# Sigmoid attention and an MLP mixer in one kernel: when keys are regrouped, and in which order keys, queries and values are loaded

## The chip, the cores and the metric

The kernel runs on one core of a Trainium2 chip. The metric is the device time of one execution in microseconds (us), as the median of several runs. An engine's name is shortened as in the profile: PE is the matmul engine, DVE the vector engine, ACT the scalar engine, POOL the general engine (it issues the loads here), SP the engine that issues stores and transposing transfers. All transfers are moved by the core's 16 DMA engines.

## The reference

For 8 batches of 12 heads, with 448 positions of 64 numbers per head, attention with a sigmoid in place of the softmax; the heads are then laid side by side (768 columns) and pass a token mixing and a channel mixing layer.

```
scores = scale * np.matmul(q, k.transpose(0, 1, 3, 2)) - np.log(S)
attn = 1.0 / (1.0 + np.exp(-scores))
x = np.matmul(attn, v)                      # then heads side by side: (8, 448, 768)
xt = x.transpose(0, 2, 1)
h = np.maximum(xt @ w_tok1, 0.0) @ w_tok2   # token mixing, 448 -> 256 -> 448
u = x + h.transpose(0, 2, 1)
h2 = np.maximum(u @ w_ch1, 0.0) @ w_ch2     # channel mixing, 768 -> 1536 -> 768
return u + h2
```

## The kernel before

Batches are counted from 0 to 7. The 12 heads of a batch are worked off in three units of four heads (u = 0, 1, 2), so there are 24 cycles, c = 3b + u. The order of all instructions on all engines is written out by hand: each engine's queue runs in the order in which the program names its instructions.

A cycle c does three things for three different units. `qk` (line 179) forms seven blocks of scores of unit c, each block followed by a sigmoid on ACT (line 191). `av` (line 201) multiplies the sigmoids of unit c - 1 with its values into two PSUM banks, 0 and 1, called xa; DVE copies them to the tile xT (line 220), and `xtrans_dma` (line 235) transposes xT through a transfer on SP to the tile xn. `tok_tail` and `tok1` (lines 260 and 278) do the first token product of unit c - 2 from its xn, and `ytrans` (line 305) the second into two banks, again 0 and 1, called yt; DVE adds them to xT and writes the tile ut (line 319). So the `av` of a cycle takes the banks that the `ytrans` at the end of the cycle before it used, once DVE has emptied them.

Between these pieces stand the products of the channel layer of earlier batches. From c = 9 on a cycle holds a third of the second channel product of batch b - 2 (lines 367 and 605); its results are added up by DVE (`o`, line 564) and stored by SP. At the end of a batch's third cycle stands the first channel product of batch b - 1 (`sevens`, line 1045, matmuls at line 491). In cycles 6 to 8 the second channel product of batch 0 stands in their place, cut into pieces that `work(share)` (line 1066) hands out in three portions a cycle. Each piece is followed by one entry of the list `copies`, if there is one, else by one of the list `early` (sums of weights on DVE, line 409).

Queries and keys reach PE in four steps. A load on POOL converts them to half precision into raw_q and raw_k (line 115). `relayout` (line 120) is a copy on DVE, one for each unit, from raw to rel (line 126). `dma_transpose` (line 138) is one transfer on SP for all three units of a batch, to the tile tr, from which `qk` reads. `through_dma(b, 0)` (line 144) makes a list of eight entries from it: three copies of k, the transpose of k, three copies of q, the transpose of q. In the loop from line 1120 the function `some(n)` runs the next n entries of that list. It is called twice in a cycle: with `within` after the third block of scores, and with `behind` after the second channel product and ahead of `ytrans`. Values need no regrouping: `av` reads raw_v.

`gated_loads(b)` (line 969) holds the loads back: a tiny copy on POOL reads the last element of the transposed queries of batch b + 1, and the loads stand behind it in POOL's queue. It is called at the end of cycles 5 and 8, inside cycle 11, and at the end of the second cycle of batches 4 to 6. raw_k and raw_q have one buffer each for these batches, raw_v has two.

In cycle 7 the list `copies` takes k's four entries ahead of the cycle's second portion of work (line 1097), in cycle 8 q's four entries after the third block of scores (line 1089).

Of the kernel before, what the change touches and what calls it, by code (L numbers as in the profile page):

```python
# [23 lines left out]
NU = 3  # L24
# [6 lines left out]
def kernel(  # L31
# [13 lines left out]
    B, H, S, E = q.shape  # L45
# [39 lines left out]
    def bank(shape, dtype, name):  # L85

        if opening_banks:
            n = opening_banks.pop(0)
        else:
            n = at_bank[0]  # L90
            at_bank[0] = (n + 1) % 4
        return pp.tile(shape, dtype, tag=f"m{n}", bufs=1, name=name)
# [7 lines left out]
    def raw_tile(b, t):  # L100
        if (b, t) not in raw:
            tag, bufs = f"raw_{t}", 2 if t == "v" else 1
            if b == 1 and t != "v":
                tag = f"rel_{t}"
            raw[b, t] = pa.tile(
                [128, NU, 2, NJ, E], FP16, tag=tag, bufs=bufs, name=f"raw_{t}_{b}"
            )
        return raw[b, t]

    def load(b, t, src, u0, u1):  # L110

        for g in range(2):
            dst = raw_tile(b, t)[64 * g : 64 * g + 64, u0:u1, :, :, :]
            heads = src[b, 6 * g + 2 * u0 : 6 * g + 2 * u1]
            nc.gpsimd.dma_start(
                out=dst.rearrange("p u hi j e -> p (u hi) (j e)"),
                in_=heads.rearrange("h (p j) e -> p h (j e)", j=NJ),
            )

    def relayout(b, t, u):  # L120

        if (b, t) not in rel:
            rel[b, t] = pa.tile(
                [128, NU, NJ, 2, E], FP16, tag=f"rel_{t}", bufs=1, name=f"rel_{t}_{b}"
            )
        nc.vector.tensor_copy(
            out=rel[b, t][:, u, :, :, :],
            in_=raw[b, t][:, u, :, :, :].rearrange("p hi j e -> p j hi e"),
        )
# [8 lines left out]
    def dma_transpose(b, t, u0, u1=NU):  # L138
        nc.sync.dma_start_transpose(
            out=tr_tile(b, t)[:, u0:u1, :, :].rearrange("e u j r -> e (u j) r"),  # L140
            in_=rel[b, t][:, u0:u1, :, :, :].rearrange("r u j hi e -> r (u j hi e)"),
        )

    def through_dma(b, u0):

        pieces = []
        for t in ("k", "q"):
            for u in range(u0, NU):
                pieces.append(lambda t=t, u=u: relayout(b, t, u))
            pieces.append(lambda t=t: dma_transpose(b, t, u0))  # L150
        return pieces

    def by_unit(b, u0):

        pieces = []
        for u in range(u0, NU):
            for t in ("k", "q"):
                pieces.append(lambda t=t, u=u: relayout(b, t, u))
            for t in ("k", "q"):
                pieces.append(lambda t=t, u=u: dma_transpose(b, t, u, u + 1))  # L160
        return pieces
# [73 lines left out]
    def xtrans_dma(b, u):  # L235
        nc.sync.dma_start_transpose(
            out=xn_tile(b, u).rearrange("s g t d -> s (g t) d"),
            in_=xTs[b % 2][:, u, :, :].rearrange("d g s -> d (g s)"),
        )
# [65 lines left out]
    def ytrans(b, u, banks=()):  # L305
        for g in range(2):
            db = NU * g + u
            if banks:
                at_bank[0] = banks[g]
            ps = bank([128, 512], FP32, f"yt_{b}_{db}")  # L310
            for tcb in range(2):
                nc.tensor.matmul(  # L312
                    out=ps[:, 0:S],
                    lhsT=h1[b, u][:, tcb, g, :],
                    rhs=w2[:, tcb, :, :],
                    start=(tcb == 0),
                    stop=(tcb == 1),
                )
            nc.vector.tensor_tensor(  # L319
                out=uts[b % 2][:, db, 0:S], in0=xTs[b % 2][:, u, g, 0:S], in1=ps[:, 0:S], op=ADD  # L320
            )
# [531 lines left out]
    def pieces_ch2(b, groups):  # L853
        for t, half in groups:
            for n in range(0, NCB, 3):
                yield 3 * DH, lambda t=t, half=half, n=n: ch2(b, t, half, n, n + 3)

    def pieces_last(b):
        for n in range(0, NCB, 3):
            yield 3 * DH, lambda n=n: ch2_last(b, n, n + 3)  # L860
# [108 lines left out]
    def gated_loads(b):  # L969

        nc.gpsimd.tensor_copy(  # L971
            out=gate[:, :], in_=tr[b + 1, "q"][:, NU - 1, NJ - 1, 126:128]
        )
        if b > 1:
            load(b + 1, "v", v, 0, NU)
        for t, src in (("k", k), ("q", q)):
            if b + 2 < B:
                load(b + 2, t, src, 0, NU)

    ON_DMA = range(N_FIRST, N_CYCLES)  # L980

# [3 lines left out]
    for c, cb in ((N_FIRST, 3), (N_FIRST + 1, 8)):  # L985
        b, u = divmod(c, NU)
        before = divmod(c - 1, NU)
        ahead = divmod(c + 1, NU)
        copies = []
# [27 lines left out]
        if u == 2:  # L1017
            copies = by_unit(2, 1)
# [33 lines left out]
    pending, copies = [], []  # L1052
    early = weight_sums()
    lane = [0]
    for c in range(2 * NU, ONE_RUN):
        b, u = divmod(c, NU)
        before, ahead = divmod(c - 1, NU), divmod(c - 2, NU)


        if c == 2 * NU:  # L1060
            first = c
            pending, shares = [*pieces_ch2(0, by_half[2:]), *pieces_last(0)], [10, 10, 10]
            total = sum(w for w, f in pending)
            spent = 0

        def work(share):
            goal = 3 * sum(shares[: c - first]) + share * shares[c - first]
            done = 0
            while pending and spent + done < total * goal / 90:
                w, f = pending.pop(0)  # L1070
                if len(pending) % 4 == 3:
                    lane[0] ^= 1
                at_bank[0] = 2 + lane[0]
                f()
                done += w
                if copies:
                    copies.pop(0)()
                elif early:
                    early.pop(0)()
            return done  # L1080

        qk(b, u, 0)
        qk(b, u, 1)
        at_bank[0] = 0
        av(*before)
        xtrans_dma(*before)
        qk(b, u, 2)
        if c == 2 * NU + 2:
            copies += through_dma(3, 0)[NU + 1 :]
        spent += work(1)  # L1090
        qk(b, u, 3)
        qk(b, u, 4)
        at_bank[0] = 0
        tok_tail(*ahead)
        tok1(*ahead, with_scores=True)
        if c == 2 * NU + 1:
            copies = through_dma(3, 0)[: NU + 1]
        spent += work(2)
        if c == 2 * NU + 2:
            utrans(b - 1)  # L1100
            token_sums(b - 1)
        qk(b, u, 5)
        qk(b, u, 6)
        if u < 2:
            at_bank[0] = 0
            ytrans(*ahead)
        spent += work(3)
        if u == 2:
            sevens(b - 1)
            at_bank[0] = 0  # L1110
            ytrans(*ahead)
            gated_loads(b)
    assert not copies and not pending and not early

    def some(n):
        for f in copies[:n]:
            f()
        del copies[:n]

    for c in range(ONE_RUN, N_CYCLES):  # L1120
        b, u = divmod(c, NU)
        before, ahead = divmod(c - 1, NU), divmod(c - 2, NU)
        if b == NU:
            within, behind = ((0, 0), (4, 2), (2, 0))[u]
        else:
            within, behind = 2, 2
        if u == 0:
            assert not copies
            copies += through_dma(b + 1, 0) if b + 1 < B else output_sums()

        X, Y = 2, 0
        at_bank[0] = X
        turn0, turn1, rest = ch2_pair(b - 2, u)
        part = len(turn1) * 2 // 3
        qk(b, u, 0)
        qk(b, u, 1)
        for f in turn0:
            f()  # L1140
        qk(b, u, 2)
        some(within)
        if c == ONE_RUN + 2:
            gated_loads(b)
        if u == 2:
            utrans(b - 1)
        at_bank[0] = Y
        av(*before, 0, 4)
        qk(b, u, 3)
        av(*before, 4, NJ)  # L1150
        xtrans_dma(*before)
        if u == 2:
            token_sums(b - 1)
        qk(b, u, 4)
        for f in turn1[:part]:
            f()
        qk(b, u, 5)
        for f in turn1[part:]:
            f()
        at_bank[0] = Y  # L1160
        tok_tail(*ahead)
        qk(b, u, 6)
        tok1(*ahead, with_scores=True)
        rest()
        some(behind)
        if u == 1 and NU < b < B - 1:
            gated_loads(b)
        if u == 2:
            at_bank[0] = Y + 1
            for w, f in pieces_last(b - 2):  # L1170
                f()
            sevens(b - 1)
        at_bank[0] = Y
        ytrans(*ahead)
# [93 lines left out]
```

## Time and profile before

| | |
|---|---|
| median of 3 runs | 347.46 us (347.26 to 347.76) |
| the profiled execution | 347.11 us |
| its span, first to last instruction | 345.3 us |
| granted PE clock over the span | 0.999 |
| DVE, ACT, POOL busy in the span | 213.7, 210.9, 56.7 us |
| PE busy in 126.32 to 165.47 us | 39.15 of 39.15 us |
| PE busy in 165.47 to 204.63 us | 39.16 of 39.16 us |
| PE busy in 204.63 to 243.78 us | 39.15 of 39.15 us |
| PE busy in 78.00 to 86.00 us | 7.89 of 8.00 us |

The stretches from 126.32 us are one batch long each (they begin with the last quarter of a second channel product). The share in which PE is busy counts modelled ends of matmuls, and so tells little of short waits inside a run of matmuls; the chain of work that ended last tells more, because in it each piece is the time from one step to the next. Between a span and the time of its run lie 1.8 us that the program's instructions do not show.

### The profile page before, as it was taken

Reading aid. Unit: us, or ns where it says so; the run is one execution under the profiler, and the core shown is the slowest. Engines: PE = TensorE matmul, PEld = TensorE weight load, DVE = VectorE, ACT = ScalarE, POOL = GpSimd, SP = SyncE. Lnnn points to the kernel's source line nnn. Section 1 sums busy time; section 2 is a strip of 40 time slices with the busy share of each in tenths; the row PEclk is TensorE's granted clock in tenths of the full one; section 3 lists DMA queues with packets and bytes.
Section 4 is the critical chain, followed back from the end, with each engine's and each line's share of the span. In section 5 each row is a group of like instructions: output and inputs, shape, how many; then the busy total and the mean of one; then the engine's idle time right before and its main releaser. Section 6 shows DMA issues by size and latency. Waiting matters only on the chain.

```text
span 345.3 us, 10256 instructions
## 1 busy us (share of the span) xinstructions
PE 338.2 (98%) x4465; PEld 241.5 (70%) x4465; DVE 213.7 (62%) x427; ACT 210.9 (61%) x271; POOL 56.7 (16%) x98
## 2 busy tenths in 40 slices
PE   7999999999999999999999999999999999999994
PEld 4555556555886679766896669766896779767962
DVE  2377466577775665756575654765665684976662
ACT  3996846487748865788448865688448875111400
POOL 8982440230040013000400013000100000000000
PEclk9999999999999999999999999999999999999999
DMA  7999999999999999989997999979963592035406
GB/s 120 174 170 189 208 203 203 169 175 219 200 181 205 198 184 208 153 126 164 181 228 87 165 193 156 199 108 170 176 135 30 82 171 68 1 78 128 79 2 159
DMA packets 104380, 52.17 MB, mean 151 GB/s; under 512 B 76432, under 2 KB 101264, under 8 KB 104336
## 3 DMA queue, kind: packets, MB, share of 16 engines
q1 hardware_dynamic: 78944, 29.70, 49.2%
q0 software_dynamic: 25168, 21.50, 41.5%
q8 instruction: 35, 0.57, 0.7%
q10 hardware_dynamic: 224, 0.33, 0.4%
q14 instruction: 9, 0.07, 0.1%
HBM read 43.45 MB, written 11.01 MB: 158 GB/s over the span
## 4 chain that ended last, share of the span: by engine, by line
PE 88%; ACT 4%; DMA 3%; DVE 2%; issue 1%; POOL 0%; DVEq 0%; ACTq 0%
PE c_ab L491 14%; PE c L367 12%; PE qk L184 9%; PE c_c L491 8%; PE xa L211 8%; PE c L605 6%; PE tk L289 5%; PE c L734 5%; PE yt L312 5%; PE c L541 4%; ACT att L191 4%; PE c L695 4%; PE c L344 3%; DMA raw_k<-in_k_dram 2%; DMA first_q<-in_q_dram 1%; PE c_b L491 1%
## 5 line engine op out<-in xcount | busy, mean ns | idle before, releaser
L191 ACT ACTIVATE att<-qk,att_bias 128x896 f16<-128x896 f32 x168 | 155.3, 1015 | 34.0 <-PE qk L184 33.7
L184 PE MATMUL qk<-tr_q,tr_k 64*64 64x448 f16 x672 | 59.5, 359 | 0.3 <-ACT att L191 0.2
L491 PEld LDWEIGHTS <-c 128*128 128x128 f16 x504 | 47.8, 98 | 1.9 <-issue 1.8
L367 PE MATMUL c<-c,h 64*64 64x384 f16 x960 | 47.1, 322 | 0.0
L220 DVE CAST xT<-xa 128x448 f16<-128x448 f32 x48 | 27.7, 620 | 31.1 <-PE xa L211 31.0
L211 PE MATMUL xa<-att,raw_v 64*64 64x448 f16 x672 | 40.3, 349 | 0.1
L512 ACT ACTIVATE pt_ab<-c_ab 128x896 f32<-128x896 f32 x21 | 19.3, 917 | 30.8 <-PE c_ab L491 30.8
L367 PEld LDWEIGHTS <-h 64*64 64x64 f16 x960 | 29.5, 107 | 11.0
L491 PEld LDWEIGHTS <-sum 128*128 128x128 f16 x378 | 36.3, 98 | 0.0
L184 PEld LDWEIGHTS <-tr_k 64*64 64x64 f16 x672 | 21.5, 105 | 19.2 <-issue 11.9
L564 DVE TENSOR_TENSOR o<-un,c 128x384 f32<-128x384 f16 x34 | 18.8, 554 | 23.9 <-PE c L605 20.6
L319 DVE TENSOR_TENSOR ut<-xT,yt 128x448 f16<-128x448 f16 x48 | 27.5, 614 | 2.5 <-PE yt L312 2.5
L211 PEld LDWEIGHTS <-raw_v 64*64 64x64 f16 x672 | 21.5, 107 | 10.6 <-issue 1.0
L971 POOL COPY gate<-tr_q 128x2 f16<-128x2 f16 x6 | 1.1, 184 | 153.0 <-DMA tr_q<-rel_q 153.0
L303 ACT ACTIVATE h<-tk 128x256 f16<-128x256 f32 x42 | 14.3, 412 | 14.8 <-PE tk L289 14.8
L541 PE MATMUL c<-c,h 128*128 128x384 f16 x120 | 22.3, 326 | 0.0
L312 PE MATMUL yt<-w,h 128*128 128x448 f16 x96 | 22.1, 353 | 0.0
L605 PE MATMUL c<-c,h 128*128 128x384 f16 x120 | 22.0, 326 | 0.0
L514 ACT ACTIVATE h<-c_ab 128x896 f16<-128x896 f32 x7 | 6.4, 917 | 24.4 <-PE c_ab L491 24.4
L289 PE MATMUL tk<-xn,w 128*128 128x256 f16 x156 | 21.2, 274 | 0.1
L521 DVE TENSOR_TENSOR h<-pt_c,c_c 128x448 f16<-128x448 f32 x21 | 13.0, 617 | 13.2 <-PE c_c L491 13.2
L521 DVE TENSOR_TENSOR h<-pt_ab,c_ab 128x896 f16<-128x896 f32 x14 | 15.2, 1084 | 9.6 <-PE c_ab L491 9.6
(100 smaller groups left out, 461.4 us busy)
## 6 DMA issues: line engine op xcount, KB each, us to landing
out_dram<-o SPq DMA_DIRECT2D x48, 192.0 KB, 2.9
c<-in_moe_w_ch_dram POOLq DMA_DIRECT2D x4, 1152.0 KB, 15.9
raw_k<-in_k_dram POOLq DMA_DIRECT2D x10, 336.0 KB, 10.8
raw_q<-in_q_dram POOLq DMA_DIRECT2D x10, 336.0 KB, 13.7
raw_v<-in_v_dram POOLq DMA_DIRECT2D x10, 336.0 KB, 8.0
out_dram<-o SPq DMA_DIRECT2D x15, 96.0 KB, 6.9
raw_q<-in_q_dram POOLq DMA_DIRECT2D x12, 112.0 KB, 5.0
raw_k<-in_k_dram POOLq DMA_DIRECT2D x12, 112.0 KB, 4.8
```

Of the source, the lines that this page charges most:

```text
L184: nc.tensor.matmul(out=ps[64 * g : 64 * g + 64, hi, 0:S], lhsT=tr[b, "k"][64 * hi : 64 * hi + 64, u, j, 64 * g : 64 * g + 64], rhs=tr[b, " ...
L191: nc.scalar.activation(out=att[b, u, j][:, :, :], in_=ps[:, :, 0:S], func=SIGMOID, bias=bias_t[:, :], scale=att_scale,)
L211: nc.tensor.matmul(out=ps[g][64 * hi : 64 * hi + 64, 0:S], lhsT=raw[b, "v"][64 * g : 64 * g + 64, u, hi, j, :], rhs=att[b, u, j][64 * g : ...
L220: nc.vector.tensor_copy(out=xTs[b % 2][:, u, g, 0:S], in_=ps[g][:, 0:S])
L289: nc.tensor.matmul(out=ps[tcb], lhsT=w1[rows, t, cols], rhs=xn[b, u][rows, :, t, :], start=(t == 0 and not with_scores), stop=(t == (2 if ...
L312: nc.tensor.matmul(out=ps[:, 0:S], lhsT=h1[b, u][:, tcb, g, :], rhs=w2[:, tcb, :, :], start=(tcb == 0), stop=(tcb == 1),)
L319: nc.vector.tensor_tensor(out=uts[b % 2][:, db, 0:S], in0=xTs[b % 2][:, u, g, 0:S], in1=ps[:, 0:S], op=ADD)
L367: nc.tensor.matmul(out=ps[p][m : m + 64, 0:n], lhsT=lhsT(p, part, m), rhs=rhs(p, part), start=(first and turn == 0), stop=(last and turn = ...
L491: nc.tensor.matmul(out=ps[:, g, p, :], lhsT=weights[n][:, d, 128 * cb : 128 * cb + 128], rhs=moving[n][:, d, :], start=(n in (1, 5, 2) and ...
L521: nc.vector.tensor_tensor(out=shaped(dst), in0=shaped(parts[gs, which]), in1=ps, op=ADD)
L541: nc.tensor.matmul(out=ps[:, 0:DH], lhsT=h2[b][:, BY_GROUP[cb], 128 * t : 128 * t + 128], rhs=c2[:, BY_GROUP[cb], cols], start=(cb == 0), ...
L605: nc.tensor.matmul(out=ps[p][:, 0:DH], lhsT=h2[b][:, BY_GROUP[n], 128 * t : 128 * t + 128], rhs=c2[:, BY_GROUP[n], DH * p : DH * p + DH], ...
```

## The change

Three things are moved, and no operation is added or left out.

```
-        if b > 1:
-            load(b + 1, "v", v, 0, NU)
         for t, src in (("k", k), ("q", q)):
             if b + 2 < B:
                 load(b + 2, t, src, 0, NU)
+        if b == 1:
+            load(3, "v", v, 0, NU)
+        elif b > 2:
+            load(b + 1, "v", v, 0, NU)
...
-        if c == 2 * NU + 1:
-            copies = through_dma(3, 0)[: NU + 1]
         spent += work(2)
...
             ytrans(*ahead)
+        if c == 2 * NU + 1:
+            copies += through_dma(3, 0)[: NU + 1]
         spent += work(3)
...
-            within, behind = 2, 2
+            within, behind = ((0, 2), (3, 3), (0, 0))[u] if b < B - 1 else (2, 2)
```

First, `gated_loads` issues k and q ahead of v, and the values of batch 3 are loaded in the call of cycle 5, behind k and q of batch 3, and no longer in the call of cycle 8. Second, in cycle 7 k's entries for batch 3 join the list after `ytrans`, ahead of the third portion of work. As entries are taken one behind each piece, this also moves what follows: on DVE two copies of k come behind cycle 7's additions to ut and the third into cycle 8, and the last copy of q comes behind the four `diffs` (line 434) of cycle 8; on SP the transpose of k moves behind xn of cycle 8 and the stores of its first outputs, and the transpose of q behind the transpose `un` (line 326) and the two stores of the last quarter of batch 0. The entries of `early` take the places that become free. Third, for batches 4 to 6 the eight entries of the list go out as none and two in the first cycle, three and three in the second, where they went out as two, two, two, two. In the first cycle of each of these batches the first two copies of k so stand in `behind`, where the third copy and the transpose of k were, and nothing in `within`; in the second cycle `within` holds the third copy of k, its transpose and the first copy of q, where two copies of q were, and `behind` the last two copies of q and its transpose, where the last copy and the transpose were.

## The prediction

> **What bounds the kernel now.** I read the page first, then the chain of waits that ended last in order of time, then DVE's, SP's and POOL's timelines around the places where that chain leaves PE.
>
> ```profile
> span 345.3 us, 10256 instructions
> PE 338.2 (98%) x4465; PEld 241.5 (70%) x4465; DVE 213.7 (62%) x427; ACT 210.9 (61%) x271; POOL 56.7 (16%) x98
> ```
>
> PE is the bound: the batches from 126.32 us on take 39.15, 39.16 and 39.15 us of matmuls without a gap, so whatever the change does counts only as PE waiting more or less. There are two waits in the change's reach. The first is in cycle 8 (chain; start, duration, what):
>
> ```profile
> 80.75 1.07 DVE ut L319 x2
> 81.81 0.04 issue
> 81.86 1.51 PE xa L211 x26
> ```
>
> `av` needs bank 1, which yt held; DVE emptied it only at 81.81, because the relayouts of k (L126) stood ahead of it and the first had waited 1.51 us for its load. The price: from the first scores of cycle 7 to its token product PE takes 72.38 to 76.05, 3.67 us, and for the same matmuls in cycle 8 80.99 to 85.14, 4.15 us. So 0.48 us are lost. The second is in cycle 11; beside it, the same piece of cycle 14 (chain):
>
> ```profile
> 120.57 0.96 PE xa L211 x16
> ...
> 159.92 0.76 PE xa L211 x16
> ```
>
> 0.20 us more, and the stretch 119.08 to 126.32 is 7.24 us where 158.43 to 165.47 is 7.04. DVE's timeline says why (first cycle 11, then cycle 14; start, duration):
>
> ```profile
> 117.21 1.21 DVE L564 TENSOR_TENSOR o<-un,c 128x384 f32<-128x384 f16 x2 [2.00 <-PE c L605]
> 118.33 1.14 DVE L126 COPY rel_q<-raw_q 128x896 f16<-128x896 f16 x2
> 119.39 1.14 DVE L319 TENSOR_TENSOR ut<-xT,yt 128x448 f16<-128x448 f16 x2
> ...
> 156.56 1.21 DVE L564 TENSOR_TENSOR o<-un,c 128x384 f32<-128x384 f16 x2 [2.00 <-PE c L605]
> 157.68 0.61 DVE L126 COPY rel_q<-raw_q 128x896 f16<-128x896 f16 x1
> 158.21 1.14 DVE L319 TENSOR_TENSOR ut<-xT,yt 128x448 f16<-128x448 f16 x2
> ```
>
> Two relayouts ahead of ut and it ends at 120.53, after `av` began at 120.40; with one it ends at 159.35, and `av` begins at 159.75. The slack is 0.40 us, a relayout's pitch 0.53 (157.68 to 158.21).
>
> **Part 1: `some` in batches 4 to 6.** `behind` stands between the products and `ytrans`. It held one copy and a transpose; now it holds two copies in the first cycle, two and a transpose in the second. That puts cycles 13, 14, 16, 17, 19 and 20 (each waits the cycle after its u = 0 or u = 1 end) where cycle 11 is now. The offsets fit: from the scores' start, ut would end 2.01 us on in cycle 13 (149.56 to 151.05 + 0.53 = 151.58, thus 2.02) and ends 2.02 us on in cycle 11 (118.51 to 120.53). Nothing covers it, PE being full: six times 0.20 = **+1.2 us**. Bounds: 0.13 a time (0.53 less 0.40, 0.8 in all) and 0.24 (half the wait of cycle 8 with its two banks, 1.4 in all). The freed `within` gives PE nothing back: in cycle 12 the xT copies at 144.87 had waited 1.14 us for PE, not DVE. k's transpose moves from 150.70 to about 152.1 and holds xn on SP to about 156.4 (154.98 now); that xn is read two cycles on, and k only in the next batch.
>
> **Part 2: k of batch 3 half a cycle later.** The wait of cycle 8 goes: without relayouts in front, ut ends by 80.8 (o at 78.7 for 0.55, a weight sum for 0.51, ut for 1.07), before `av` at 81.4. **-0.48 us**, if nothing is late next. SP's queue is late next (start, duration of the issues):
>
> ```profile
> 77.31 4.05 SPq L577 DMA_DIRECT2D out_dram<-o  x4
> 81.47 5.38 SPq L139 DMA_TRANSPOSE tr_k<-rel_k  x1
> 86.95 1.25 SPq L236 DMA_TRANSPOSE xn<-xT  x1
> 88.29 1.19 SPq L577 DMA_DIRECT2D out_dram<-o  x2
> 89.58 4.80 SPq L139 DMA_TRANSPOSE tr_q<-rel_q  x1
> 94.42 3.74 SPq L326 DMA_TRANSPOSE un<-ut  x1
> 98.26 1.20 SPq L766 DMA_DIRECT2D out_dram<-o  x2
> ```
>
> One transpose occupies SP for 3.2 to 5.4 us. Now k starts at 81.47, q at 89.58, and q lands 6.8 us on, at 96.4, 5.6 us before the scores of batch 3 want it (chain: 101.98). Afterwards the order is xn, stores, k, un, stores, q. xn can start when xT is done, 84.2, and takes 1.25; the stores 1.2: k starts at 86.7. It takes 5.4 as before (the transfers queued before it, stores and xn, end about 5.4 us later in either case; see part 3): 92.1. un 3.7: 95.9 with gaps. Stores 1.2: 97.2. q between 3.24 (its shortest issue, 121.12) and 4.8, say 4.0: 101.2, and it lands 2.0 us after its issue ends (94.38 to 96.4): **103.2**. Scores could have started at 101.98 - 0.48 = 101.50. They start at 103.25, **+1.3 us** against now, and the 0.48 is swallowed. Bounds: with k issued in 3.75 (112.82) and q in 3.24 it lands at 100.7, in time, and -0.48 remains; with k held 2 us more and q at 4.8 it lands at 106, +4.1.
>
> By bytes, as a second way: xn moves 256 KB, a transpose of k or q 672, un 768, an output tile's two stores 384, a load of k, q or v 672 in half precision. Between 81.8 (the later of q's loads, issued at about 73.8, landing 8.0 us on) and 88.87 (k transposed: 81.47 + 7.4) some 1.5 MB went through, 215 KB a us. Afterwards v of batch 3 comes too: about 4.5 MB from 81.8 to q's landing (the end of xn 80 KB, four and two stores 768 and 384, v 672, xn 256, k 672, un 768, stores 192, q 672), 20.8 us, 102.6. The two ways agree. The Trainium skill's page "DMA: Bandwidth & Descriptors" (Latency and other measured facts) gives transposes 261 GB/s; by that the 2.1 MB of k, un and q would take about 8 us, q would land near 101 and the sum of this part would be -0.48; the trace shows about 215, and the trace decides.
>
> **Part 3: loads.** The gate of batch 3's end opens at 96.49 because q landed; it moves to 103.3. Behind it stand k and q of batch 4, no longer behind v: k lands 6.75 us after the gate's first load (71.84 to 78.59), thus at 110.6, and is copied at 111.09 + 1.3; q at about 114, copied at 119.6. Both in time. v of batch 3 goes in at 74.5, after q's issue, when its buffer is free (last read 65.84). It competes with xn of cycle 7, which was issued at 75.97, landed 7.6 us later at about 83.5 and is wanted at 85.14 (84.66 without the wait). Sharing the engines, it lands at 84 to 85.2; should all of v (672 KB at 215, 3.1 us) go first, 86.6. Either is followed by the later wait for q, and so swallowed by it: 0. The xn issued at 106.97 lands 8.2 us on, at 115.17, and PE wants it at 115.29. It now travels with the later k and q loads: 0 to 0.8 us, I take **+0.2**, as the bytes left ahead of it are about the same (0.8 to 0.9 MB). In batches 4 to 6 v lands last of three, near 184 instead of 174 in batch 4 (168.54 + 14.7 for the last load now); it is read at about 190. Free.
>
> **Sum:** 1.3 + 0.2 + 1.2 = +2.7 us on a span of 345.3 and a run of 347.11. That run is 0.35 below the median 347.46, so the median goes to **350.2**; 348.9 to 351.8 is this case's own range (q landing at 102 to 104.8).
>
> **Rivals.** *SP keeps up.* q lands by 101.5, and 0.48 is gained; only the relayouts cost. For it: unhurried issues of 3.24 and 3.75; against: 5.38 and 4.80 at this very place. -0.48 + 1.2: 348.2. *The relayouts fit in*, the other side: the wait for the yt banks costs under 0.08 a time, which takes a DVE pitch under 0.43, since slack is 0.40; then six waits cost less than the 0.48 gained, and with q in time nothing is left to pay: 347.0 at no cost at all. For it: the slack of 0.40. Against it: cycle 11, a copy of the case. *PE's clock falls* at the wait for q. The rows show full clock (1.00) where PE stood for 1.40 us of the first 5, and 0.92 in the last stretch, 340.00 to 345.30, with 4.40 us idle; a stall of 4 us (q at 106) with such a dip, 8% of 5.3 us: 4.1 + 0.4 + 0.2 + 1.2 = 5.9, so 353.4. The Trainium skill's page "TensorE: Matmul & The Clock Gate" (What's actually happening) has the clock halved after an idle window of some 3.4 us, which would add about 1.7 us of its own; no run here shows a halved clock. *v ahead of xn*: the loads take precedence in cycle 8 and delay everything on SP's transfers behind it, q landing 0.7 later, at 103.9: 2.0 + 0.2 + 1.2 gives 350.9.
>
> **How the numbers follow.** Forecast 0.62, SP keeps up 0.18, relayouts fit 0.08, clock 0.06, v ahead 0.06. A change under 0.2% (0.7 us) can't be told from none here: 346.8 to 348.2 is "same". Half of 0.18, 0.05 of 0.08 and 0.02 of the forecast's low tail lie there: 0.16. Faster has the other 0.03, slower 0.81. The range 347.4 to 352.6 leaves out the third case and the fourth, and takes in q between 100.7 and about 105.3.
>
> **What would show it.** Cycle 8's xa without the 0.49 of idle before it; SP issuing un and two stores ahead of q; q landing near 103 and the first scores of batch 3 waiting for it, with the gate near 103.3; in cycles 13, 14, 16, 17, 19 and 20 xa pieces of 0.96 for 0.76, batches of 39.5 us. I am wrong if q lands by 101.5, or if those batches stay at 39.15.

## The result, and the profile after

| | before | changed |
|---|---|---|
| median of 6 runs each | 347.36 us (346.32 to 349.41) | 352.26 us (351.80 to 353.75) |
| ratio | | 1.0147, 95% interval 1.0109 to 1.0185 |
| profiled execution, its span | 347.11, 345.3 us | 352.62, 350.9 us |
| granted PE clock over the span | 0.999 | 0.995 |

The change made the kernel slower by some 5 us. The two spans differ by 5.6 us, and the chain places them: batch 1's first channel product starts at 93.45 us where it started at 89.04, which is +4.4, and the three batches from 130.73 us on take 39.55, 39.54 and 39.55 us where they took 39.15, 39.16 and 39.15, which is +1.2. The ratios below leave out runs that took over 1.5% more than the fastest of their kernel.

The larger part is one wait. The list of waits of the changed kernel has this on PE (who waits, for what: us in total, times, longest):

```profile
PE tk L270 <- DMA xn<-xT: 3.2, 1, 3.2
```

The chain of the changed kernel around it (start, duration, what):

```profile
75.72 12.18 DMA xn<-xT
87.90 0.04 issue
87.95 0.30 PE tk L270 x4
88.25 1.19 PE tk L289 x6
89.44 2.06 PE c L734 x12
91.50 0.68 PE qk L184 x6
92.19 1.10 PE c L734 x12
```

The xn that cycle 7 sent off took 12.18 us; in the kernel before it took 7.6. PE stood still until it landed. What followed ran slowly. The same work in the chain of the kernel before:

```profile
85.31 0.11 PE tk L270 x4
85.42 0.76 PE tk L289 x6
86.18 1.09 PE c L734 x12
```

Six matmuls at line 289 took 1.19 us where they took 0.76, and twelve at line 734 took 2.06 where they took 1.09. The stretches of the changed kernel have the reason (per stretch: length, then busy time of PE, PEld, DVE, ACT, POOL; PE clock, DMA share, GB/s):

```profile
86.00:88.00 2.00, 0.05 (x4) 0.05 (x4) 1.93 (x5) 0.62 (x1) 0.00 (x0) 1.00 1.19 292
88.00:90.00 2.00, 2.00 (x14) 1.06 (x16) 0.76 (x2) 0.77 (x2) 0.00 (x0) 0.61 1.25 279
90.00:92.00 2.00, 2.00 (x18) 0.73 (x14) 0.00 (x0) 0.00 (x0) 0.00 (x0) 0.54 1.03 303
92.00:94.00 2.00, 2.00 (x29) 1.50 (x26) 0.51 (x1) 1.88 (x2) 0.00 (x0) 1.00 1.28 290
```

After the standstill the clock granted to PE is 0.61 and 0.54 for two stretches of 2 us. From cycle 8's token product to the channel product PE needs 5.50 us (87.95 to 93.45), before 3.73 (85.31 to 89.04): 1.8 us for the clock. With the wait of 3.2 and less the 0.5 that the kernel before lost to the yt banks in this cycle, that is the 4.4, but for rounding.

The smaller part is where the relayouts went. The chain in cycles 13 and 14 of the changed kernel, and the starts of two last quarters of a second channel product, whose difference is a batch's length:

```profile
130.73 2.07 PE c L734 x24
...
156.03 0.95 PE xa L211 x16
...
164.53 0.95 PE xa L211 x16
...
170.28 2.07 PE c L734 x24
```

The value products that took 0.76 us take 0.95, twice a batch: 0.40 us for each of three batches.

In the new order SP issues q behind un and the stores, and the gate opens late (SP's timeline of the changed kernel, then POOL's):

```profile
88.23 4.52 SPq L139 DMA_TRANSPOSE tr_k<-rel_k  x1
92.80 4.45 SPq L326 DMA_TRANSPOSE un<-ut  x1
97.35 1.18 SPq L766 DMA_DIRECT2D out_dram<-o  x2
98.57 3.37 SPq L139 DMA_TRANSPOSE tr_q<-rel_q  x1
```

```profile
103.92 0.19 POOL L971 COPY gate<-tr_q 128x2 f16<-128x2 f16 x1 [28.30 <-DMA tr_q<-rel_q]
```

q landed just ahead of 103.92, but PE asked for it only at 106.39, as PE was late already.

### The profile page after: what moved, and what is told of

It is laid out like the page before. It is cut to its first block, busy times and chain, and to the rows that moved or that the text cites. A ratio compares the mean times of both kernels' runs of the same rounds, so it can differ in the third digit from the quotient of the medians.

```text
span 350.9 us, 10254 instructions
## 1 busy us (share of the span) xinstructions
PE 340.7 (97%) x4465; PEld 244.2 (70%) x4465; DVE 213.3 (61%) x427; ACT 211.7 (60%) x271; POOL 56.6 (16%) x98
## 4 chain that ended last, share of the span: by engine, by line
PE 88%; DMA 5%; ACT 4%; DVE 1%; issue 1%; DVEq 0%; ACTq 0%
PE c_ab L491 14%; PE c L367 12%; PE qk L184 9%; PE xa L211 8%; PE c_c L491 8%; PE c L605 6%; PE tk L289 5%; PE c L734 5%; PE yt L312 5%; PE c L541 5%; ACT att L191 4%; PE c L695 4%; DMA xn<-xT 3%; PE c L344 3%; DMA first_q<-in_q_dram 1%; PE c_b L491 1%
## 5 line engine op out<-in xcount | busy, mean ns | idle before, releaser
L184 PE MATMUL qk<-tr_q,tr_k 64*64 64x448 f16 x672 | 63.4, 360 | 0.3 <-ACT att L191 0.2
L367 PE MATMUL c<-c,h 64*64 64x384 f16 x960 | 48.2, 322 | 0.0
L211 PE MATMUL xa<-att,raw_v 64*64 64x448 f16 x672 | 41.3, 350 | 0.0
L367 PEld LDWEIGHTS <-h 64*64 64x64 f16 x960 | 31.8, 107 | 10.3
L184 PEld LDWEIGHTS <-tr_k 64*64 64x64 f16 x672 | 24.3, 106 | 18.6 <-issue 12.2
L211 PEld LDWEIGHTS <-raw_v 64*64 64x64 f16 x672 | 22.7, 107 | 10.7 <-issue 2.1
## 6 DMA issues: line engine op xcount, KB each, us to landing
raw_q<-in_q_dram POOLq DMA_DIRECT2D x10, 336.0 KB, 10.9
```

Of the source, the lines that this page charges most:

```text
L184: nc.tensor.matmul(out=ps[64 * g : 64 * g + 64, hi, 0:S], lhsT=tr[b, "k"][64 * hi : 64 * hi + 64, u, j, 64 * g : 64 * g + 64], rhs=tr[b, " ...
L211: nc.tensor.matmul(out=ps[g][64 * hi : 64 * hi + 64, 0:S], lhsT=raw[b, "v"][64 * g : 64 * g + 64, u, hi, j, :], rhs=att[b, u, j][64 * g : ...
L367: nc.tensor.matmul(out=ps[p][m : m + 64, 0:n], lhsT=lhsT(p, part, m), rhs=rhs(p, part), start=(first and turn == 0), stop=(last and turn = ...
```

## The experiments

Theory A was formed on this profile: the load of batch 3's values, now on the DMA engines together with k and q of batch 3, holds up the xn of cycle 7. Rival B: that xn is late because the stores of cycle 7, which had waited behind the relayouts of k, go out earlier. Each ratio is against the kernel before, run beside it.

### One part of the change at a time

**Values of batch 3 early, nothing else.**

```
-        if b > 1:
+        if b > 2:
             load(b + 1, "v", v, 0, NU)
...
+        if b == 1:
+            load(3, "v", v, 0, NU)
```

> Kernel before with one part of the change: the values of batch 3 are loaded behind k and q of batch 3; k's regrouping and the pieces of batches 4 to 6 stay. Theory A (the load of v holds up the xn of cycle 7 on the shared DMA engines): xn issued near 76 lands at 86 to 89 instead of 83.5, PE waits for it 1 to 3.5 us in cycle 8, the clock granted dips below 1.00 behind the wait, and the total is 2 to 5 us over the kernel before. Rival B (xn is late because the stores of cycle 7, no longer held back by the relayouts, go out a microsecond earlier): here the stores are where they were, so xn lands near 83.5 and the time is that of before within 0.3 us.

Ratio 1.0053 (1.0023 to 1.0083), about 1.8 us: the early load costs time by itself, a little under the lower end of what was expected. xn of cycle 7 took 11.9 us and landed at 88.0, as theory A has it, with the stores where they were. That the load alone made it so late this one execution does not show, because its transfers were slow before these values were issued at 74.02: a load of batch 2's values, which landed at 74.38, took 7.5 us where it took 4.8 before. The wait for xn was only 0.9 us, since PE came later: the first relayout of k waited 3.00 us for its load (1.51 before), and the value product of cycle 8 waited 0.8 us for the banks behind it. The clock stayed at 1.00 around the wait, where a dip was expected.

**k of batch 3 later, nothing else.**

```
-        if c == 2 * NU + 1:
-            copies = through_dma(3, 0)[: NU + 1]
         spent += work(2)
...
             ytrans(*ahead)
+        if c == 2 * NU + 1:
+            copies += through_dma(3, 0)[: NU + 1]
         spent += work(3)
```

> Kernel before with only k of batch 3 regrouped half a cycle later. Theory A: xn of cycle 7 lands near 83.5, no wait for it; the 0.5 us of the wait for the yt banks in cycle 8 are gained, unless q, issued behind un and two stores, lands after 101.5: by the prediction's count at 103 (+1.3 us instead of -0.5), by what the changed kernel showed of q's issue (3.4 us, landing 5.2 us on) in time, -0.5 us. Rival B: xn lands late as in the changed kernel, +2 to +4.5 us.

Ratio 1.0142 (1.0072 to 1.0212): as slow as the whole change, and for a reason that neither theory named. The chain of this kernel:

```profile
96.95 5.19 DMA tr_q<-rel_q
102.14 0.14 issue
102.28 0.57 PE qk L184 x8
...
107.56 10.85 DMA xn<-xT
118.41 0.04 issue
118.45 0.34 PE tk L270 x4
```

xn of cycle 7 was in time (7.2 us) although the stores of cycle 7 went out early here, against rival B. q landed at 102.14 and cost a wait of 0.6. But the gate stands behind q: the loads of v, k and q that began at 97.0 in the kernel before began at 102.8, and now travelled with the xn of cycle 9, which took 10.85 us instead of 8.2. PE waited 2.6 us for it in cycle 10, and the clock fell to 0.50 behind that.

**The changed kernel with batch 3's values back at their old place.**

```
+        if b == 2:
+            load(b + 1, "v", v, 0, NU)
         for t, src in (("k", k), ("q", q)):
             if b + 2 < B:
                 load(b + 2, t, src, 0, NU)
-        if b == 1:
-            load(3, "v", v, 0, NU)
-        elif b > 2:
+        if b > 2:
             load(b + 1, "v", v, 0, NU)
```

> Changed kernel with one part undone: the values of batch 3 are again loaded ahead of k and q of batch 4. Theory A: the 4.4 us of the wait for xn and of the slow clock go; what is left is +1.2 for the relayouts and -0.5 for the wait in cycle 8, or +1.3 if q is late: +0.7 to +2.5 us against before. Rival B: still +4 to +5.6 us.

Ratio 1.0150 (1.0101 to 1.0199). Both halves of the expectation failed: the xn of cycle 9 took 11.6 us (a wait of 3.2), as with k alone, and the xn of cycle 7 took 10.6 us (a wait of 1.6) although v was not beside it. Up to cycle 8 this program issues the same work in the same order as the one with k alone, whose xn took 7.2: the same transfer lands 3.4 us apart in two executions. So this xn is late in all three profiles with the values loaded early (table below), and sometimes late without them.

**The pieces of batches 4 to 6, nothing else.**

```
-            within, behind = 2, 2
+            within, behind = ((0, 2), (3, 3), (0, 0))[u] if b < B - 1 else (2, 2)
```

> Kernel before with only the pieces of batches 4 to 6 shared out as in the change. Six waits of 0.20 us for the yt banks, batches of 39.55 instead of 39.15 us: +1.2 us. If those waits were made by the loads' new order instead, 0.

The profile has it: batches of 39.55, 39.54 and 39.55 us (127.70 to 167.25 to 206.79 to 246.34). The times don't: ratio 0.9994 (0.9969 to 1.0019), where +1.2 us, a ratio of 1.0035, was expected. The runs of this kernel and of the one before spread by 3 us; so a larger dose was tried.

**Three relayouts ahead of the sums instead of two.**

```
-            within, behind = 2, 2
+            within, behind = ((0, 3), (0, 5), (0, 0))[u] if b < B - 1 else (2, 2)
```

> Kernel before with three relayouts ahead of the token product's sums in the first and the second cycle of batches 4 to 6, where the change has two. If the wait for the yt banks sets their price, each wait grows from 0.20 by a relayout's pitch of 0.53 to 0.73 us, a batch takes 40.6 us, and the time is 4.4 us over the kernel before. If PE has slack there, under 1 us.

Ratio 1.0137 (1.0096 to 1.0179), 4.8 us. The chain, at the starts of three last quarters:

```profile
128.15 2.07 PE c L734 x24
...
168.75 2.07 PE c L734 x24
...
209.35 2.07 PE c L734 x24
```

40.60 us a batch, 1.45 more than before for two waits: 0.72 each, 0.53 more than with two relayouts, as expected. Each relayout beyond the slack is paid in full. The whole span of this profile is 6.1 us longer than before and not 4.4: PE is 1.8 us late already where the first of these batches starts (128.15 for 126.32), after a wait of 1.9 us for weights at 32 us, in a stretch that is the same in both kernels.

### The clock

**The wait filled with matmuls.** 27 products of constants ahead of `tok_tail` in cycle 8 of the changed kernel, into a bank that nobody reads.

```
+        if c == 2 * NU + 2:
+            at_bank[0] = 0
+            heat[0] = bank([128, 512], FP32, "heat8")
+            for _ in range(27):
+                nc.tensor.matmul(
+                    out=heat[0][:, 0:256],
+                    lhsT=ident[:, :],
+                    rhs=c2[:, 0, 0:256],
+                    start=True,
+                    stop=True,
+                )
         at_bank[0] = 0
         tok_tail(*ahead)
```

> Changed kernel with 27 matmuls of 256 columns on constants ahead of cycle 8's token product, into a bank that nobody reads; the output is the same. They fill some 2.9 us of the wait for xn. If the clock falls because PE stands idle, the granted clock stays at 1.00 from 86 to 94 us, the 1.7 to 1.8 us that the matmuls behind the wait took longer go, and the time falls by about that against the changed kernel, to 350.0 to 351.0. If the clock has another cause, or the slow matmuls were waiting for something else, they stay slow and the time is that of the changed kernel.

351.20 us, ratio 1.0104 (1.0062 to 1.0145). The same stretch as above, in this kernel:

```profile
90.00:92.00 2.00, 2.00 (x30) 0.99 (x27) 0.00 (x0) 1.03 (x2) 0.00 (x0) 1.00 1.13 331
```

The clock stays at 1.00, and from the token product to the channel product PE needs 3.93 us (88.38 to 92.31) instead of 5.50. The standstill made the clock fall. Of the 1.6 us about 1.1 arrive in the median, a little less than expected: PE now comes to batch 3's scores sooner and waits 0.8 us for q. The two medians are of different sessions, and the intervals of the two ratios overlap, so the 1.1 is rough.

### Versions that keep the transfers apart

**The changed kernel, with batch 3's values loaded once the xn of cycle 7 has landed.**

```
         xtrans_dma(*before)
+        if c == 2 * NU + 1:
+            nc.gpsimd.tensor_copy(out=gate[:, :], in_=xn[before][:, 1, 3, 126:128])
+            load(3, "v", v, 0, NU)
```

> Changed kernel, but the load of batch 3's values stands in POOL's queue behind a copy that reads the xn of cycle 7, so it can't compete with that transpose, and is still done before the loads of batch 4. Theory A (xn of cycle 7 and of cycle 9 are late only where loads share the DMA engines with them): xn of cycle 7 lands at 83 to 85 with no wait or one under 0.7 us, xn of cycle 9 near 6 us after its issue as in the changed kernel, q of batch 3 at 103 to 104.5 and a wait for it of 1 to 2.5 us; in all +1 to +3.5 us on the kernel before, 2 to 4 us under the changed kernel. Rival B (the stores going out earlier delay xn): xn of cycle 7 lands at 86 or later and PE waits over 1.5 us for it.

Ratio 1.0193 (1.0145 to 1.0241), no faster than the change, where +1 to +3.5 us was expected. xn of cycle 7 took 8.9 us, landed near 84.4, and PE hardly waited; xn of cycle 9 took 5.9. Now q paid (list of waits on PE, then SP's timeline):

```profile
PE qk L184 <- DMA tr_q<-rel_q: 4.6, 1, 4.6
```

```profile
86.58 8.65 SPq L139 DMA_TRANSPOSE tr_k<-rel_k  x1
95.27 3.86 SPq L326 DMA_TRANSPOSE un<-ut  x1
99.23 1.18 SPq L766 DMA_DIRECT2D out_dram<-o  x2
100.46 3.35 SPq L139 DMA_TRANSPOSE tr_q<-rel_q  x1
```

With v beside it the issue of k's transpose held SP for 8.65 us, un and the stores followed, and q landed at 105.7; behind the wait of 4.6 us the clock fell to 0.53. The wait that the prediction had put first is real as soon as xn's is taken away.

**q's transpose ahead of un.** The kernel before with k later, but in cycle 8 the list is emptied ahead of `utrans`; one relayout fewer ahead of the sums of cycle 10.

```
         spent += work(2)
+        if u == 2:
+            while copies:
+                copies.pop(0)()
...
-            within, behind = ((0, 0), (4, 2), (2, 0))[u]
+            within, behind = ((0, 0), (4, 1), (3, 0))[u]
```

> Kernel before with k of batch 3 regrouped half a cycle later, but q's last copy and its transpose ahead of un and of the stores of batch 0's last quarter, and one relayout fewer ahead of the sums in cycle 10; all loads as before. If regrouping k later costs time because q's transpose stands behind un and the stores, and with it the gate of batch 4's loads, then here q lands near 97, the gate opens near 97, the xn of cycle 9 is no later than in the kernel before, and the 0.5 and 0.2 us of cycles 8 and 11 are gained: 0.3 to 1 us under it. If the later relayouts of k cost by themselves, 2 us or more over it, as with k alone regrouped later.

347.57 us, ratio 0.9999 (0.9971 to 1.0026), and not the 0.3 to 1 us less that were expected. The gate of this kernel (POOL's timeline):

```profile
96.53 0.19 POOL L971 COPY gate<-tr_q 128x2 f16<-128x2 f16 x1 [22.58 <-DMA tr_q<-rel_q]
```

It opens where it did before, and the 1.4% of k regrouped later are gone: what made it cost was q behind un and the stores. The 0.5 and 0.2 us were gained (the value product of cycle 8 took 1.32 us, that of cycle 11 0.76), and given back: the xn of cycle 9 took 9.4 us, a wait of 1.0.

**The same with batch 3's values behind the xn of cycle 7.**

```
-        if b > 1:
+        if b > 2:
             load(b + 1, "v", v, 0, NU)
...
         xtrans_dma(*before)
+        if c == 2 * NU + 1:
+            nc.gpsimd.tensor_copy(out=gate[:, :], in_=xn[before][:, 1, 3, 126:128])
+            load(3, "v", v, 0, NU)
```

> Kernel before with k of batch 3 regrouped half a cycle later, q's last pieces ahead of the transpose un, batch 3's values loaded behind the xn of cycle 7, and in cycle 10 one relayout ahead of the token product's sums in place of two. Theory A: no wait for xn in cycles 8 and 10, q of batch 3 lands before 100, the 0.5 us of cycle 8 and the 0.2 of cycle 11 are gained: 0.5 to 1.5 us under the kernel before. If xn is late all the same: 1 us or more over it.

Ratio 1.0001 (0.9966 to 1.0036), where 0.5 to 1.5 us less were expected. In its profile no xn is waited for, and the span is 345.1; the xn of cycle 9 took 8.6 us and landed when PE wanted it. The runs behind the ratio spread from 345.42 to 350.59 us.

**That version, with batch 4's queries behind the xn of cycle 9.**

```
-            if b + 2 < B:
+            if b + 2 < B and (b, t) != (2, "q"):
                 load(b + 2, t, src, 0, NU)
...
         xtrans_dma(*before)
+        if c == ONE_RUN:
+            nc.gpsimd.tensor_copy(out=gate[:, :], in_=xn[before][:, 1, 3, 126:128])
+            load(4, "q", q, 0, NU)
```

> The version before this one (k of batch 3 later, q's last pieces ahead of un, values of batch 3 behind the xn of cycle 7, one relayout fewer ahead of the sums in cycle 10), and now also the load of batch 4's queries held back until the xn of cycle 9 has landed. Theory A (the xn of cycle 9 is late because batch 4's loads share the DMA engines with it): that xn lands in 4 to 6.5 us instead of 8.2 to 11.6, at least 2 us before PE wants it, the runs spread less, and the median is 0.7 to 2 us under the kernel before. If the spread has another source (the first 60 us), the xn lands early all the same, and median and spread stay.

Ratio 1.0178 (1.0105 to 1.0250), where a gain was expected. That xn took 5.0 us, as theory A has it, but the queries came at 123.4: their relayout held DVE, behind it the sums, behind these the value product of cycle 11, which waited 4.8 us. With the two held-back loads alone, and k regrouped as before:

> Kernel before with the two held-back loads alone (values of batch 3 behind the xn of cycle 7, queries of batch 4 behind the xn of cycle 9); k's regrouping and all relayouts stay. Theory A: no wait for either xn; the 0.5 us of cycle 8 and 0.2 of cycle 11 stay; 0 to 1.3 us under the kernel before, and 0.5 to 0.8 over the version with both. If holding the values back makes q of batch 3 late, PE waits for it at the start of batch 3.

Ratio 1.0059 (1.0021 to 1.0096) from seven of its twelve runs, where a gain was expected; the other five took 354.84 to 357.13 us. Its profile is of one of those five, so its lines are not compared.

**Queries of batch 4 behind the xn of cycle 10, used at the end of cycle 11.** Against the version with batch 4's queries behind the xn of cycle 9; the loads of batches from 4 on go k, q, v besides.

```
-            within, behind = ((0, 0), (4, 1), (3, 0))[u]
+            within, behind = ((0, 0), (4, 0), (0, 4))[u]
...
-        if c == ONE_RUN + 2:
-            gated_loads(b)
...
-        if c == ONE_RUN:
+        if c == ONE_RUN + 1:
             nc.gpsimd.tensor_copy(out=gate[:, :], in_=xn[before][:, 1, 3, 126:128])
             load(4, "q", q, 0, NU)
...
         some(behind)
+        if c == ONE_RUN + 2:
+            gated_loads(b)
```

> As the version that held batch 4's queries back behind the xn of cycle 9, but they are loaded behind the xn of cycle 10 and regrouped only at the end of cycle 11, where no sums for the next value product wait behind them; loads of batch 5 go k, q, v behind that. If a late transfer is what costs, and a later use gives the stretch from 72 to 115 us room: no wait for xn in cycles 8, 10 and 11, none for the values' banks, 0.5 to 2 us under the kernel before. If the transfers merely collide elsewhere: a wait for q's load at the end of cycle 11 or for k of batch 5 in cycle 12, and 1 us or more over it.

Ratio 1.0173 (1.0146 to 1.0200). No xn was waited for. The load of q was (DVE's timeline):

```profile
131.66 1.67 DVE L126 COPY rel_q<-raw_q 128x896 f16<-128x896 f16 x3 [5.48 <-DMA raw_q<-in_q_dram]
```

DVE waited for it with the sums of the last quarter's output in its queue, and the first channel product wanted the bank of these: a wait of 4.9 us. No version tried is faster than the kernel before by more than the noise.

The time of an xn (256 KB) from issue to landing, by what was sent into the queues beside it:

| xn of | beside it | us |
|---|---|---|
| cycle 7 | k, q and v of batch 3 | 12.2, 11.9, 11.9 |
| cycle 7 | k and q of batch 3 | 7.6 in the kernel before, 5.1 to 10.6 in nine others |
| cycle 9 | v, k and q of batch 4 | 8.2, 8.2, 9.3, 9.4, 10.9, 11.6 |
| cycle 9 | k and q of batch 4 | 5.2, 5.9, 6.1, 7.2, 8.6 |
| cycle 9 | k of batch 4 | 5.0, 6.6 |

## Why the prediction was right, and where it was wrong

The direction was right, the size was not: 350.2 was forecast and 352.26 measured, inside the range of 347.4 to 352.6, 0.3 us under its upper end. That it lies inside is luck: the upper part of the range stood for a late q, and what filled it was a late xn and a slow clock, which the forecast had at nothing. Of the signs that the prediction named, the longer batches, the order on SP and the gate near 103.3 came; a wait of batch 3's scores for q did not.

*Part 1, the relayouts: right to the digit in the profile.* Six waits of 0.20 us were forecast, and the batches are 0.40 us longer each; three relayouts show the slope of 0.53. In the times of the kernel with these pieces alone the 1.2 us did not show, and why is open.

*Part 2, the wait in cycle 8: right.* The 0.5 us are gained, in every version that moves the relayouts.

*Part 2, q behind SP's queue: the landing was right, the wait was not there.* 103.2 was forecast and the gate opened at 103.92. That the sum came out is in part luck, as its items differ and their errors cancel: k's transpose could only start at 88.23 (86.7 forecast), since the issue of xn ahead of it took 2.55 us for 1.25, and then took 4.5 for 5.4; un took 4.5 for 3.7, q's issue 3.4 for 4.0. PE wanted q at 106.39, not 101.50, so +1.3 was 0 here. With the xn in time q is waited for, 0.6 and 4.6 us in two experiments. The second way of the prediction, by bytes, agrees less well than it says: it has the later of q's loads land 8.0 us on, which is the mean of the two, while that load took 8.8 and landed at 82.6. From there its bytes give some 240 KB a us and q near 101, an estimate on the other side of the 101.5 from which q would be late.

*Part 3, the xn of cycle 7: the step that failed.* It said "Either is followed by the later wait for q, and so swallowed by it: 0", with a landing of 84 to 85.2, or 86.6 if all of v went first. It landed at 87.9, beyond that bound, with v itself landing 12.4 to 14.9 us after its issue. The bound let v pass alone at 215 KB a us; in the trace all that was in flight took longer, the four stores behind xn too (10.7 to 11.6 us for 5.8 to 7.8). And the swallowing went the other way: the wait for xn was the larger, and took q's into itself. In place of 1.3 stand 3.2 for the wait, 1.8 for the clock and 0.5 off, some 4.4.

*Part 3, the xn of cycle 9: +0.2 was forecast, 0 came (6.1 us),* as v was no longer among the loads beside it. Where v is still among them and the gate is late, in the kernel with k alone later, this xn with its slow clock and a wait of 0.6 us for q costs about what the whole change costs. So the early values take away the collision that the later k makes in cycle 10, and the changed kernel has one in cycle 8 in its place.

*The rivals.* "PE's clock falls" had the mechanism and put it at the wrong wait: priced at 0.4 us from the last stretch, it cost 1.8. The 0.92 of that stretch, from which the price was taken, is a mean that hid the half clock: from 344.50 to 345.30 us the granted clock of the kernel before is 0.50. The estimate from the Trainium skill's page "TensorE: Matmul & The Clock Gate" (What's actually happening), half a clock and about 1.7 us, was the better one: the trace shows 0.54, and 1.8 us. "v ahead of xn" had the load that did it, but let it delay q, at 2.0 us, with no wait for xn and no slow clock. "SP keeps up" and "the relayouts fit in" fell.

What stays open: what makes the same xn land 3.4 us apart in two executions of the same order, and so how much of the 12.2 us is due to the values and how much to such a spread; and where the spread of the kernel before comes from (346.1 to 349.9 us beside the version with q ahead of un). One candidate lies ahead of all that the change moves: near 32 us PE waits for weights of a channel product (line 344), not at all in the profile before, 0.6 us in that of the pieces of batches 4 to 6, 1.9 us in that of three relayouts. That transfers have no slack between 72 and 115 us is a reading of these runs: of the four versions that held a load back and whose profiles are compared, three paid with a late transfer (that load, or q's transpose), and one had an xn land just in time. It was not measured by itself.

## What to carry to other kernels

Before moving a load, list each transfer that is in flight beside it and the moment its reader wants it; a transfer with 1.6 us to spare is the one to price, and it is to be priced with all that is issued into its window, not only with what stands ahead of it in its own queue. A wait that is hidden by another is not gone: sum up by the latest of the two, and work out which is the later before calling one of them free. If a matmul engine may stand still for about 2 us or longer, add a slower clock behind it: here a standstill of 1.9 us was enough once, and one of 1.6 us was not.

## What the runs showed of the hardware

The clock granted to PE fell to 0.50 to 0.54 in 2-us stretches behind standstills of 1.9, 2.6, 3.2 (twice), 4.6, 4.8 and 4.9 us. It stayed at 1.00 behind standstills of 0.9 and 1.6 us, and where one of 3.2 was filled with matmuls. The shortest is the wait for weights in the kernel with three relayouts (waits on PE, then a stretch behind it; the wait ends at 34.09 us):

```profile
PE c L344 <- DMA c<-in_moe_w_ch_dram: 1.9, 1, 1.9
```

```profile
36.00:38.00 2.00, 2.00 (x9) 0.74 (x6) 0.00 (x0) 1.91 (x2) 2.00 (x5) 0.51 1.17 212
```

The page of the Trainium skill named above puts the idle time that halves the clock at a free-running window of some 3.4 us; here 1.9 us were enough once.

One transposing transfer of 256 KB, the xn of cycles 7 and 9, took from 5.0 to 12.2 us, on the whole longer with more beside it, though 7.2 and 10.6 us were both measured with the same beside it. An issue can hold SP's queue longer too: with k regrouped late, the issue of its transpose took 6.44 to 9.14 us in the four versions that sent off batch 3's values from 83 to 86 us, just ahead of it, and 4.15 to 4.52 us in the others.
